# Attention and experts on one core: the third value products of every second unit moved beside the first two, and the first slot's transposes six steps earlier

## The chip, the cores and the metric

The kernel runs on one core of one Trainium2 chip. The metric is device time in microseconds (us) of one execution; less is better. The core has five engines with a queue each: PE (TensorE, matrix products), DVE (VectorE), ACT (ScalarE), POOL (GpSimd) and SP (which here issues DMAs). An instruction waits in its queue for what it needs, and everything behind it in that queue waits too.

## The reference

```python
def _attn_ref(q, k, v, g_q, g_k):              # q, k, v: 8 batches, 12 heads, 448 tokens, 64
    q_n, k_n = (rmsnorm(q, g_q), rmsnorm(k, g_k))
    scores = scale * np.matmul(q_n, k_n.transpose(0, 1, 3, 2))
    scores = scores - np.max(scores, axis=-1, keepdims=True)
    attn = np.exp(scores)
    attn = attn / (np.sum(attn, axis=-1, keepdims=True) + 1e-09)
    return np.matmul(attn, v)
...
def _moe_ref(x, modality_id, w_gate, modality_bias, w1, w2):   # x: 3584 tokens of 768
    logits = x @ w_gate + modality_bias[modality_id]
    e_idx = np.argmax(logits, axis=1)          # one of 8 experts
    ...
    for e in range(E):
        h = np.maximum(x[mask] @ w1[e], 0.0)   # w1: 768 x 1024, w2: 1024 x 768
        out[mask] = gate_w[mask, None] * (h @ w2[e])
```

The output of the attention, with its heads side by side, is the `x` of the second part. All is float32.

## The kernel before

**Attention.** A unit is two heads of one batch, 48 units in all. The 896 rows of its two heads are seven chunks of 128 key rows (j = 0 to 6; chunk 3 holds rows of both heads). The main loop (line 1425) counts steps `n = 7 i + j`: in the step (i, j) PE makes the scores of chunk j of unit i, already transposed (`st`, line 1012: a product in one pass and a second one with the low halves), ACT takes their exponential into `p` (line 1023), and around these two stands the work of other units that a plan assigned to the step. That plan is written out by hand: `put(n, ...)` files a piece of work under a step (lines 1395 to 1423), from the numbers of `PLAN` (line 34). On each engine the instructions run in the order in which the loop issues them.

The pieces that matter here, with the step at which they stand in the main part:

- `sa` (line 981): scores of a later unit (two units ahead), one chunk a step, only for their row maxima; DVE reduces each (line 994). Its PSUM pool has two buffers, so an `sa` needs the reduction of the `sa` two before it.
- `st` has two PSUM buffers too: it needs the exponential of the step two before it.
- `tr` (line 902): transposes of normalised q and k, in steps 3 and 0; ACT casts the result, DVE takes the low half.
- `av` (line 1051): value products. For each of the chunks c = 0, 1, 2 it makes two products, one for each head (chunks c and 4 + c of `p`), each 64 columns of the array wide, side by side. For c = 3 it is one product of full width. `PLAN['av'] = (1, 1, 4, 6)` puts unit u's c = 0 and 1 into step 1 of unit u + 1, c = 2 into step 4, c = 3 into step 6. A float32 product of this kind leaves two records, so c = 0 and 1 together are eight.
- `mt` (line 999), step 1: the row maxima turned for the subtraction.
- `sums` and `gates` (lines 1078, 1087), 32 columns wide, four side by side: `sums` in step 4 of even units, `gates` in step 4 of units 5, 9, 13 and so on, right behind the `av` of that step.
- `xt` (line 1122), step 4: transposes of the finished output of an earlier unit; DVE scales and stores it.
- routing of a finished batch: small DVE instructions (`route`, `route_top` with six of them, line 1163, and others) that a list called `slow` hands out between the steps; `route_top` only in step 4.

**Experts.** Tokens are gathered into slots of 256 of one expert. A slot is a first product with `w1` (`mm1_half`, line 604, tile `ph`, eighteen products for each half column block), a relu, and a second with `w2` (`mm2_step`, `py`). Weights and tokens are split into high and low parts by an ACT cast and a DVE subtraction (`split1`, `w1w`). The first slot starts while attention ends: its tokens are fetched by `xfetch(0)` at n = 312 (line 1534) in four DMAs, and `xturn(0, g)` (line 575) turns them in three groups: DVE transposes 32x32 blocks into a scratch area of `r2w` (one area for all three groups), then ACT casts that to `xh` and DVE subtracts for `xl` (both in `xw`). Each group's cast and subtraction are filed one step behind its transposition. After the loop (line 1566), PE goes on with `mm1_half(0, 0, 0)`, which needs all three groups, the last unit's `av`, and so on.

Of the kernel before, what the change touches and what calls it, by code (L numbers as in the profile page):

```python
# [21 lines left out]
NJ = 7  # L22
NP = H // 2
NU = B * NP
# [42 lines left out]
def kernel(  # L67
# [507 lines left out]
    def xturn(s, g):  # L575
        tt = view(r2w, PW + VW + W, 128, 2, 8, 32) if s == 0 else view(yw, 512 * g, 128, 2, 8, 32)
        V.transpose(out=tt.rearrange("p c g j -> p g c j"),
                    in_=xv(s).rearrange("p g (i c) -> p g c i", c=6)[:, :, 2 * g : 2 * g + 2])
        tt = tt.rearrange("p c g j -> p c (g j)")

        def cast():
            A.copy(xh[:, 2 * g : 2 * g + 2], tt)
            V.tensor_tensor(out=xl[:, 2 * g : 2 * g + 2], in0=tt,
                            in1=xh[:, 2 * g : 2 * g + 2].bitcast(F32), op=ALU.subtract)

        return cast
# [222 lines left out]
    if True:  # L809
# [543 lines left out]
        post, fin = {}, {}  # L1353
# [3 lines left out]
        def at(where, n, fn):  # L1357
            where.setdefault(n, []).append(fn)
# [16 lines left out]
        def put(n, *what):  # L1375
            plan.setdefault(n, []).append(what)

        P = PLAN
        AVJ, XTJ, XTE, SMJ, LAJ, RCJ = (P[x] for x in ("av", "xt", "xte", "sm", "la", "rc"))
        LD0, XRJ = 0, (1, 3, 5)  # L1380
        XTB, XCB, XTB0, XCB0 = (6, 7, 8), (9, 10, 13), (9, 10, 11), (12, 13, 15)
        XLB, XFB = (2, 5), 7
        W3B = (6, 8, 10, 12, 13, 14)
# [11 lines left out]
        for u in range(NU):  # L1395
            for j in range(NJ):
                jj = ((0, 1, 2, 4, 5, 6, 3) if u < P["early"] else (3, 0, 1, 2, 4, 5, 6))[j]
                put(when("sa", u) + j * (P["sastep"] if u == 0 else 1), "sa", u, jj)
            put(when("mt", u), "mt", u)
            if u < NU - 1:  # L1400
                for c in range(4):
                    put(NJ * (u + 1) + (AVJ[c] if u < NU - 2 else min(AVJ[c], 6)), "av", u, c)
            put(xt_at(u), "xt", u)
            if u % 2:
                put(NJ * (u + 1) + (SMJ if u < NP * (B - 2) else P["sml"]), "sums", u - 1)
            if u % 4 == 3:
                put(NJ * (u + 2) + (LAJ if u < NP * (B - 2) else min(LAJ, 4)), "gates", u // 4)
                put(NJ * (u + 2) + (RCJ if u < NP * (B - 2) else min(RCJ, 6)), "recips", u // 4)
            put(when("tk", u), "tr", u, 1)
            put(when("tq", u), "tr", u, 0)  # L1410
            put(when("nq", u), "norm", u, 0)
            put(when("nk", u), "norm", u, 1)
            put(when("sk", u), "sq", u, 1)
            put(when("sq", u), "sq", u, 0)
            if ("rs", u) in P["first"]:
                put(when("rs", u), "rs", u // 3, P["rs0"].get(u, 0), u % 3 + 1)
            elif u > 8 and u % 3 == 2:
                put(when("rs", u), "rs", u // 3, 0, 3)
            if 5 < u < 10:
                put(when("ld", u), "load", u)  # L1420
            elif u > 9 and u % 2 == 0:
                put(when("ld", u) - 1, "load", u, 2, (0,))
                put(when("ld", u) + 1, "load", u, 2, (1,))

        for n in range(P["start"], NJ * NU):
            i, j = divmod(n, NJ)
# [43 lines left out]
            if puts and n >= puts[0][0] and n - lastput[0] >= 3:  # L1470
                lastput[0] = n
                puts.pop(0)[1]()
            if i == NU - 1 and j in XRJ:
                at(post, n + 1, xturn(0, XRJ.index(j)))
            run(pre["A"], n)
            run(pre["V"], n)
            pump(P["rush"][0] if state["rush"] else P["pmpa"][j], j)
# [82 lines left out]
        u, g = NU - 1, NU // 4 - 1  # L1560
# [52 lines left out]
        for s in range(NSTAT):  # L1613
# [32 lines left out]
            for b_ in range(16):  # L1646
                t, j = divmod(b_, 8)
# [100 lines left out]
```

## Time and profile before

| | |
|---|---|
| median of three timed runs | 1034.56 us (1033.47 to 1035.49) |
| profiled execution, its own time | 1032.14 us |
| span of that execution in the trace | 1030.4 us |
| busy: PE / DVE / ACT / POOL | 98% / 72% / 69% / 69% of the span |
| mean granted clock of TensorE | 0.998 of full speed |

Times in rows are microseconds from the start of the span. Attention lasts to about 535 us, the expert slots from there to the end. Matmuls are pipelined, and a record's end is modelled: from start to start is what one costs when the engine is full. A start that stands a few hundredths behind the one ahead belongs to an instruction that is queued behind it.

### The profile page before, as it was taken

The page shows a single profiled execution, that of the slowest core. Times are in us where ns is not written, and L with a number is a line of the kernel's source. Part 1 is how long each engine was busy: PE and PEld are TensorE (multiplying, and loading weights), DVE is VectorE, ACT ScalarE, POOL GpSimd, SP SyncE. Part 2 cuts the span into 40 slices and gives each one's busy share as a digit, 9 for nine tenths or more (in the row PEclk, how much of TensorE's full clock was granted, in tenths as well). Part 3 has the DMA queues.
Part 4 walks back from the last instruction along what each step waited for, and adds up shares of the span by engine and source line. Part 5 has one row for each costly group of instructions (what it writes and reads, how often), then busy time and mean ns, then how long its engine had stood idle before and what let it go on. Part 6 is the DMA issues. An engine that isn't in the chain of part 4 may idle for free. (4 is left out here: it accounts for less than half of the span.)

```text
span 1030.4 us, 18867 instructions
## 1 busy us (share of the span) xinstructions
PE 1013.8 (98%) x6462; PEld 818.4 (79%) x6462; DVE 744.3 (72%) x1260; ACT 709.1 (69%) x1379; POOL 706.2 (69%) x747
## 2 busy tenths in 40 slices
PE   9999999999999999999999999999999999999997
PEld 7655666666666666656559999999999999999995
DVE  6778888887888788887777986855675567656740
ACT  7897999989989899888655555645564455545531
POOL 7887888888798887889866656655544554565351
PEclk9999999999999999999999999999999999999999
DMA  8775667868777686756928516224572342234162
GB/s 205 200 164 125 163 151 177 175 138 186 166 166 159 162 190 150 165 113 138 263 91 270 89 30 201 79 62 124 162 270 71 113 124 82 63 103 123 43 209 92
DMA packets 147900, 148.20 MB, mean 144 GB/s; under 512 B 72702, under 2 KB 137682, under 8 KB 147284
## 3 DMA queue, kind: packets, MB, share of 16 engines
q1 hardware_dynamic: 122398, 105.08, 42.6%
q0 software_dynamic: 25328, 41.82, 12.9%
q8 instruction: 53, 0.87, 0.4%
q14 instruction: 51, 0.42, 0.2%
q10 hardware_dynamic: 70, 0.02, 0.0%
HBM read 150.31 MB, written 33.39 MB: 178 GB/s over the span
## 5 line engine op out<-in xcount | busy, mean ns | idle before, releaser
L609 PE MATMUL ph<-xw,w1w 128*128 128x256 f32 x2016 | 246.2, 283 | 1.7 <-ACT xw L52 1.0
L609 PEld LDWEIGHTS ph<-xw,w1w 128*128 128x128 f32 x2016 | 243.9, 192 | 3.4 <-ACT xw L52 1.2
L52 DVE TENSOR_REDUCE at_hlw<-sa 128x1 f32<-128x448 f32 x336 | 205.2, 619 | 26.0 <-PE sa L991 24.1
L1019 PE MATMUL st<-w1w 128*128 128x448 f32 (+1 forms) x480 | 183.5, 431 | 1.3 <-ACT r2w L52 0.9
L52 POOL DMA_INDIRECT r<-in_moe_w_dram,tb_w x60 | 79.1, 1318 | 56.8 <-DVE w1w L52 41.5
L52 ACT ACTIVATE hhw<-ph 128x512 fp32r<-128x512 f32 x56 | 33.5, 598 | 121.0 <-PE ph L609 121.0
L639 PE MATMUL py<-w2lw,hhw 128*128 128x384 f32 x448 | 113.7, 334 | 0.0
L52 ACT ACTIVATE r2w<-st 128x448 f32<-128x448 f32 x168 | 91.1, 545 | 32.7 <-PE st L1019 25.9
L52 DVE TENSOR_TENSOR w1w<-r,w1w 128x768 fp32r<-128x768 f32 x112 | 104.5, 963 | 11.8 <-ACT w1w L52 10.5
L52 POOL DMA_INDIRECT r2w<-in_moe_w_dram,tb_vi x48 | 48.5, 1010 | 91.7 <-DVE w2lw L52 83.6
L991 PE MATMUL sa<-w1w 128*128 128x448 f32 (+1 forms) x288 | 108.0, 375 | 1.9 <-DVE at_hlw L52 1.5
L52 ACT CAST w1w<-xw 64x448 fp32r<-64x448 f32 x188 | 105.7, 562 | 3.7 <-issue 1.4
L52 DVE TENSOR_TENSOR w2lw<-r2w,w2ha 128x1536 fp32r<-128x1536 f32 x28 | 49.1, 1757 | 81.3 <-ACT w2ha L52 81.3
L1019 PEld LDWEIGHTS st<-w1w 128*128 128x128 f32 (+1 forms) x480 | 86.0, 190 | 24.4 <-issue 11.1
L1019 PE MATMUL st<-w1w,w2ha 65*128 65x448 f32 x288 | 100.4, 369 | 0.0
L52 ACT ACTIVATE at_w2lw<-st 128x448 f32<-128x448 f32 x168 | 90.7, 545 | 12.1 <-PE st L1019 7.0
L52 POOL TENSOR_TENSOR xrw<-r,at_hlw 112x512 f32<-112x512 f32 x95 | 97.6, 1048 | 0.5
L52 POOL TENSOR_TENSOR r2w<-r2w 128x448 f32<-128x448 f32 (+1 forms) x72 | 83.0, 1152 | 21.5 <-DVE r2w L52 15.1
L52 ACT CAST w1w<-r 128x768 fp32r<-128x768 f32 x112 | 95.3, 904 | 0.1
L52 ACT ACTIVATE yw<-py,ltn 128x384 f32<-128x384 f32 x55 | 29.4, 579 | 79.2 <-PE py L639 75.6
L639 PEld LDWEIGHTS py<-w2lw,hhw 128*128 128x128 f32 x448 | 80.9, 188 | 0.0
L52 POOL TENSOR_TENSOR r2w<-r2w,at_w2lw 64x448 f32<-64x448 f32 (+1 forms) x48 | 55.0, 1145 | 30.0 <-DVE r2w L52 15.6
(303 smaller groups left out, 2203.5 us busy)
## 6 DMA issues: line engine op xcount, KB each, us to landing
w1w<-xw SPq DMA_DIRECT2D x216, 112.0 KB
xrw<-xg SPq DMA_DIRECT2D x56, 192.0 KB
xg<-xrw SPq DMA_DIRECT2D x13, 768.0 KB
r<-in_q_dram SPq DMA_DIRECT2D x19, 448.0 KB
r<-in_k_dram SPq DMA_DIRECT2D x19, 448.0 KB
w2ha<-xw SPq DMA_DIRECT2D x72, 112.0 KB
w1w<-w1w SPq DMA_DIRECT2D x48, 112.0 KB
r2w<-in_v_dram SPq DMA_DIRECT2D x24, 224.0 KB
```

Of the source, the lines that this page charges most:

```text
L52: return fn(*a, **kw)
L609: PE.matmul(ps[:, i], lhsT=lt_, rhs=rt_[:, c], start=n == 0, stop=n == 17)
L639: PE.matmul(ps[n][:, :384], lhsT=lt_[:, j, 128 * t : 128 * t + 128], rhs=rt_[:, 384 * n : 384 * n + 384], start=j == 0 and m == 0, stop=j ...
L991: PE.matmul(ps[:, :S], lhsT=t["qq"][r, h, a : a + 128], rhs=t["kk"][h][r], start=True, stop=True)
L1019: PE.matmul(ps[:, :S], lhsT=l, rhs=t["qq"][:, h] if first else t["ql"][0:65, h], start=first and (j != 3 or h == 0), stop=not first and (j ...
```

## The change

The value products of chunk c = 2 of the even units 8 to 44 (nineteen units) are filed under step 1 of the following unit, with those of c = 0 and 1, instead of step 4. The three transpositions of the first slot's tokens, with their casts and subtractions, stand at n = 324, 326, 328 instead of 330, 332, 334: in steps 2, 4 and 6 of unit 46 instead of steps 1, 3 and 5 of unit 47.

```diff
-        LD0, XRJ = 0, (1, 3, 5)
+        LD0, XRN = 0, (324, 326, 328)
...
                 for c in range(4):
-                    put(NJ * (u + 1) + (AVJ[c] if u < NU - 2 else min(AVJ[c], 6)), "av", u, c)
+                    aj = AVJ[1] if c == 2 and u % 2 == 0 and 8 <= u < 45 else AVJ[c]
+                    put(NJ * (u + 1) + (aj if u < NU - 2 else min(aj, 6)), "av", u, c)
...
-            if i == NU - 1 and j in XRJ:
-                at(post, n + 1, xturn(0, XRJ.index(j)))
+            if n in XRN:
+                at(post, n + 1, xturn(0, XRN.index(n)))
```

PE's queue in steps 1 to 4 of unit 23, before (the number behind a name is the program's own; `sa_1` to `sa_4` are for unit 25):

```order
L1061 MATMUL av_3344<-r2w,at_w2lw 64x448 x4
L1002 MATMUL mt_3349<-idn,at_hlw 7x128
L1019 MATMUL st_2_3359<-w1w 128x448 x2
L991 MATMUL sa_1_3362<-w1w 128x448
L1019 MATMUL st_3_3375<-w1w 128x448 x4
L991 MATMUL sa_2_3380<-w1w 128x448
L910 MATMUL tr_0_3382<-idn,xrw 128x112 x4
L1019 MATMUL st_4_3390<-w1w 128x448 x2
L991 MATMUL sa_4_3393<-w1w 128x448
L1061 MATMUL av_3344<-r2w,at_w2lw 64x448 x2
L1127 MATMUL xt_3397<-idn,at_hlw 112x128 x4
```

The same place now:

```order
L1061 MATMUL av_3344<-r2w,at_w2lw 64x448 x6
L1002 MATMUL mt_3351<-idn,at_hlw 7x128
L1019 MATMUL st_2_3361<-w1w 128x448 x2
L991 MATMUL sa_1_3364<-w1w 128x448
L1019 MATMUL st_3_3377<-w1w 128x448 x4
L991 MATMUL sa_2_3382<-w1w 128x448
L910 MATMUL tr_0_3384<-idn,xrw 128x112 x4
L1019 MATMUL st_4_3392<-w1w 128x448 x2
L991 MATMUL sa_4_3395<-w1w 128x448
L1127 MATMUL xt_3397<-idn,at_hlw 112x128 x4
```

Two of the six products have moved up past the score products of three steps, three products for row maxima and two sets of transposes; the output transposes follow `sa_4` directly. On DVE, ACT and POOL nothing moves in these units.

ACT's queue at the end of attention, before, from unit 46's fourth step (`st_3_6264` is unit 46; `st_0_6312` to `st_2_6335` are unit 47):

```order
L52 ACTIVATE r2w<-st_3_6264 128x448
L52 ACTIVATE r2w<-st_4_6272 128x448
L52 CAST w1w<-r_0_158 128x768
L52 ACTIVATE r2w<-st_5_6294 128x448
L52 ACTIVATE r2w<-st_6_6304 128x448
L52 COPY xrw<-av_6239 128x448
L52 ACTIVATE lo_6246<-lo_6246 112x32
L52 ACTIVATE at_w2lw<-st_0_6312 128x448
L52 ACTIVATE at_w2lw<-st_1_6323 128x448
L52 CAST w1w<-r_1_159 128x768
L52 ACTIVATE at_w2lw<-st_2_6335 128x448
L52 CAST xw<-r2w 128x512
```

And now:

```order
L52 CAST xw<-r2w 128x512
L52 ACTIVATE r2w<-st_4_6275 128x448
L52 CAST w1w<-r_0_158 128x768
L52 ACTIVATE r2w<-st_5_6298 128x448
L52 CAST xw<-r2w 128x512
L52 ACTIVATE r2w<-st_6_6310 128x448
L52 COPY xrw<-av_6239 128x448
L52 ACTIVATE lo_6246<-lo_6246 112x32
L52 ACTIVATE at_w2lw<-st_0_6319 128x448
L52 CAST xw<-r2w 128x512
L52 ACTIVATE at_w2lw<-st_1_6332 128x448
L52 CAST w1w<-r_1_159 128x768
```

The three casts of the turned tokens (`xw<-r2w`) stand ahead of exponentials of units 46 and 47 that they stood behind; the exponential of `st_3` is the one ahead of the first row. On DVE the three transpositions move in the same way; now:

```order
L52 TENSOR_TENSOR w1w<-r_0_158,w1w 128x768
L52 STREAM_TRANSPOSE r2w<-xrw 128x8x2x32
L52 TENSOR_TENSOR yw<-xt_6254,rs_171 112x4x128
L52 TENSOR_TENSOR xw<-r2w,xw 128x512
L52 STREAM_TRANSPOSE r2w<-xrw 128x8x2x32
L52 TENSOR_REDUCE ra_6286<-lo_6246 112x4
L52 TENSOR_TENSOR ra_6286<-lo_6246,ra_6286 112x32
L52 SCALAR_TENSOR_TENSOR cd_6287<-ra_6286,ie_132 112x32
L52 TENSOR_REDUCE ra_6286<-cd_6287 112x4
L52 TENSOR_TENSOR zb_134<-i_e,ra_6286 112x32
L52 TENSOR_TENSOR lo_6246<-lo_6246,ra_6286 112x32
L52 TENSOR_TENSOR w1w<-r_0_158,w1w 128x768
```

Before, the first transposition stood behind this second weight subtraction, the output scaling, a partial sum and a count; it has moved up past eleven instructions, to right behind the first weight subtraction.

## Rows read from the trace of the kernel before

**Rows 1.** The page: the span, and busy time of each engine.
```profile
span 1030.4 us, 18867 instructions
PE 1013.8 (98%) x6462; PEld 818.4 (79%) x6462; DVE 744.3 (72%) x1260; ACT 709.1 (69%) x1379; POOL 706.2 (69%) x747
```

**Rows 2.** PE's timeline, unit 21, step 4: start us, us, line, op, out<-in, [idle before <-releaser].
```profile
252.96 0.37 PE L991 MATMUL sa<-w1w 128*128 128x448 f32 x1
253.26 0.97 PE L1061 MATMUL av<-r2w 128*64 128x448 f32 x4
254.16 0.56 PE L1090 MATMUL sm<-at_hhw,wg 128*32 128x448 f32 x1
```

**Rows 3.** PE's timeline, unit 23, step 4.
```profile
274.42 0.37 PE L991 MATMUL sa<-w1w 128*128 128x448 f32 x1
274.72 0.97 PE L1061 MATMUL av<-r2w,at_w2lw 128*64 128x448 f32 x4
275.63 0.65 PE L1127 MATMUL xt<-idn,at_hlw 128*112 128x128 f32 x4
276.03 0.65 PE L1019 MATMUL st<-w1w 128*128 128x448 f32 x2
```

**Rows 4.** PE's timeline near the end of attention: xt between full-width products.
```profile
514.62 0.37 PE L1019 MATMUL st<-w1w,w2ha 65*128 65x448 f32 x1
514.83 0.60 PE L1127 MATMUL xt<-idn,at_hhw 128*112 128x128 f32 x4
515.19 0.64 PE L1019 MATMUL st<-w1w 128*128 128x448 f32 x2
```

**Rows 5.** PE's timeline: a run of eight value products and the last unit's twelve.
```profile
259.25 1.72 PE L1061 MATMUL av<-at_w2lw 128*64 128x448 f32 x8
...
533.81 2.48 PE L1061 MATMUL av<-at_w2lw 128*64 128x448 f32 x12
```

**Rows 6.** DVE's timeline, unit 23 from step 4, and one reduction of unit 40.
```profile
274.76 0.62 DVE L52 TENSOR_TENSOR w1w<-tr,xw 128x448 fp32r<-128x448 f32 x1 [0.33 <-ACT xw L52]
...
275.83 0.18 DVE L52 TENSOR_REDUCE ra<-lo 112x4 f32<-112x32 f32 x1
...
277.53 0.61 DVE L52 TENSOR_REDUCE at_hlw<-sa 128x1 f32<-128x448 f32 x1
...
458.85 0.61 DVE L52 TENSOR_REDUCE at_hlw<-sa 128x1 f32<-128x448 f32 x1
```

**Rows 7.** PE's timeline: the first sa of unit 24 and of unit 41.
```profile
278.50 0.37 PE L986 MATMUL sa<-xw 128*128 128x448 f32 x1
...
459.51 0.47 PE L986 MATMUL sa<-xw,w2ha 128*128 128x448 f32 x1 [0.42 <-DVE at_hlw L52]
```

**Rows 8.** PE's timeline: unit 47's steps 3 and 4, then the first slot's products.
```profile
524.31 1.47 PE L1019 MATMUL st<-w1w 128*128 128x448 f32 x6
...
529.62 1.69 PE L609 MATMUL ph<-xw,w1w 128*128 128x256 f32 x12 [0.40 <-ACT at_w2lw L52]
532.30 0.38 PE L609 MATMUL ph<-xw,w1w 128*128 128x256 f32 x1 [0.98 <-ACT xw L52]
533.02 0.86 PE L609 MATMUL ph<-xw,w1w 128*128 128x256 f32 x5 [0.34 <-DVE xw L52]
```

**Rows 9.** DVE's timeline at the end of attention: two weight subtractions, the first transposition.
```profile
514.36 0.96 DVE L52 TENSOR_TENSOR w1w<-r,w1w 128x768 fp32r<-128x768 f32 x1 [0.36 <-ACT w1w L52]
...
518.67 1.90 DVE L52 TENSOR_TENSOR w1w<-r,w1w 128x768 fp32r<-128x768 f32 x1 [1.40 <-ACT w1w L52]
...
522.11 1.12 DVE L52 STREAM_TRANSPOSE r2w<-xrw 128x512 f32<-128x512 f32 x1
```

**Rows 10.** ACT's timeline: unit 47's first two exponentials, the first cast of turned tokens.
```profile
521.61 0.97 ACT L52 ACTIVATE at_w2lw<-st 128x448 f32<-128x448 f32 x2
...
524.65 0.61 ACT L52 CAST xw<-r2w 128x512 fp32r<-128x512 f32 x1
```

**Rows 11.** SP's queue: the four DMAs that fetch the first slot's tokens.
```profile
499.97 2.02 SPq L563 DMA_DIRECT2D xrw<-xg  x4
```

## Prediction, made before the changed kernel ran

> **What bounds the kernel now.** The first thing to read is the share of busy time [rows 1]: PE is busy for 1013.8 of 1030.4 us, so PE's own stream is the bound and only what shortens that stream, or makes it wait, moves the end. The timeline of PE inside the attention steps comes next, because the change rearranges it. A value product (av, line 1061) runs in a narrow tile 64 columns wide, and the rows show what one visit to that mode costs. In unit 21 a row-maximum product (sa) starts at 252.96, the av behind it at 253.26, the gate product behind that at 254.16 [rows 2]: entering takes 0.30 us from start to start, the pair itself 0.90. In unit 23 there is no gate product, and the visit stands alone between sa and the output transposes (xt): 274.42, 274.72, 275.63, 276.03 [rows 3]. Then DVE and ACT must be read in the same steps: the next product that needs a buffer from them is what takes over when PE gets faster. Last comes the end of attention, where the first expert slot's products (ph) stop three times [rows 8].
>
> **Joining the third chunk.** Each moved pair leaves step 4 of an odd unit and lengthens the av run in step 1 of the same unit. What it adds: the run of eight records lasts 1.72 us, the one run of twelve (unit 47's own, at the end) 2.48 [rows 5], so +0.76. What it removes depends on the neighbour. With gates behind it (units 9, 13 to 45: ten units) the narrow mode is still entered for the gates, so 0.30 stays, and 254.16 - 253.26 = 0.90 goes: net -0.14. With xt behind it (units 11, 15 to 43: nine units) the whole visit goes. 276.03 - 274.42 = 1.61 becomes what full-width products show in unit 47, 514.62 to 514.83 to 515.19 = 0.57 [rows 4]: -1.04, net -0.28. On PE alone this is 10 x 0.14 + 9 x 0.28 = 3.9 us.
>
> No wait comes in with it: the pair needs the exponentials of the unit's sixth and earlier steps, and the score product two places ahead of it in PE's queue needs the last of them already, for its PSUM buffer. What it moves is the rest of the unit. Between step 1 and step 4 everything on PE now stands 0.76 later, and ACT and DVE with it; after step 4 PE is 0.28 ahead again. The price is in those two engines.
>
> **What DVE does with the 0.76.** In unit 23, DVE's subtraction at 274.76 waits for ACT (0.33 idle), ACT's cast for PE; so this chain starts 0.76 later. Behind it come a row maximum, six routing instructions from 275.83, the scaled output and the next row maximum, 277.53 to 278.14, with no gap between them [rows 6]. PE's sa of the next unit needs the buffer that this reduction frees; it starts at 278.50 [rows 7], a slack of 0.36. Now the reduction ends at 278.14 + 0.76 = 278.90, and a reduction that ended at 459.46 let its sa start at 459.51 [rows 6, 7], so sa cannot start before 278.95. That is 0.45 later than before, in place of 0.28 sooner. The trace has the same seven instructions between the two reductions, with a slack of 0.35 to 0.36, in five of the nine units: 11, 15, 23, 27, 35. In the other four (19, 31, 39, 43) routing stands elsewhere: that reduction follows PE's own product directly, with more than twice the slack, so DVE holds nothing there. ACT has four casts between its exponentials of steps 4 and 5 and is late by about 0.14 in two of those four, as I put its rows one behind the other from the delayed start. In the ten units with gates step 4 keeps about the length that it has today in the nine others, and no routing stands in it, so neither engine holds PE.
> Sum: 5 x 0.45 - 4 x 0.28 + 2 x 0.14 - 10 x 0.14 = 2.25 - 1.12 + 0.28 - 1.40 = 0.0 us. Bounds: -3.9 if nothing holds PE; +1.0 if the hold is 0.2 longer than read.
>
> **The transposes, six steps sooner.** Before, ph runs twelve products from 529.62, then stops 0.98 for ACT and 0.34 for DVE on the last third of its transposed block, after 0.40 at its start for an exponential that stood behind two casts of that work; it reaches av at 533.81 [rows 5, 8]. Eighteen products at 0.12 each and the entry of 0.2 would take 2.3 instead of 4.2, so 1.9 goes if the block is ready. It will be: the first transposition follows the weight subtraction that ends at 515.32 and takes 1.12 [rows 9]; the instructions that the order now puts between, laid end to end with their own rows' durations and a cast of 0.61 ahead of each subtraction [rows 10], end the third transposition at 523.6 and its last subtraction near 526, before 529.6.
> The cost is on ACT, whose queue is in order. The third cast now stands ahead of unit 47's second exponential, which ran right behind the first from 521.61 [rows 10]. It waits for the transposition at 523.6, so this exponential starts near 524.1 (2.0 later), and a 0.9 weight cast and the next exponential follow. PE needs them for the six score products that begin at 524.31 [rows 8], the first four and then the last two: about 0.3 and 0.5 of waiting, 0.8 in all. Of it the 0.40 before ph is taken back. ph starts near 529.95 instead of 529.62, and av follows 2.25 later, at 532.2: -1.6, taken as -1.5. Bounds: -2.3 if ACT's delay is all hidden; -0.6 if the second weight subtraction, now at 520.8, takes 1.90 as its row did and not 0.96 as the first [rows 9], since the transposition waits behind it. I take 0.96: POOL has no work there after the move.
> The Trainium skill (SBUF — State Buffer, SBUF: two separate sides) says that DVE and POOL lock each other out of a shared port pair when DVE reads two SBUF inputs. By that rule the 1.90 is a POOL instruction's doing; this trace fits it, and were POOL to meet the moved subtraction, the part would bring the 0.6 named above.
> The moved block's loads are not moved: four parts are issued at 499.97 to 501.99 [rows 11], which left 20 us to the first transposition at 522.11 and leaves 13 now.
>
> **Sum.** 0.0 - 1.5 = -1.5 us, that is 1030.6 beside the profiled execution's 1032.14. That execution lies 2.4 under the median of the three timed runs, 1034.56, so I carry the difference: **1033.1**. What follows after 534 is PE's unbroken stream, and starts earlier as a whole.
>
> **Rivals.** A: DVE does not hold PE, and the whole 3.9 arrives: 1034.56 - 3.9 - 1.5 = 1029.2. For it: over the whole span PE stood for DVE's maxima hardly at all. Against: the slack of 0.36 is read in five units, and 0.76 + 0.28 is three times that. The Trainium skill (TensorEngine Tiling (Array Packing), Key Properties) says that a change of tiling mode drains TensorE; by that rule alone, each mode change saved is a gain, which is this rival. The entry of 0.30 agrees with the drain, but the rule does not see DVE.
> B: the transposes bring nothing, since ACT's delay of 2.0 meets PE in full and takes back the 1.5: 1034.6. For it: PE has two score buffers only. Against: PE needs that exponential at 524.31 and it ended by 522.58 before, a margin of 1.7 to set against the 2.0.
> C, the other side: the block's loads land late. The first transposition would then hold DVE from 515.3, ACT's cast behind it and PE's sixth step of unit 46 behind that. PE's margin there is about 1.4, beyond it each us costs one; the forecast turns to slower by over 0.2% when the last part lands after 515.3 + 1.4 + 3.6 = 520.3, 18 us after its issue: 1037. Against: no DMA wait stands at 522.11, and the queue's traffic is no heavier before.
>
> **How the numbers follow.** Forecast 0.70 (its own range 1031.0 to 1034.6), A 0.17, B 0.08, C 0.05. About 0.2% (2.07 us) is what a measurement of this kernel can tell from no change. The forecast is 1.5 under, and with its own bounds about 0.19 of its 0.70 lies beyond 2.07; with A that makes faster 0.36; slower is C, 0.05; the rest, 0.59, is no difference. The range reaches down over A's value, from 1028.9 to 1034.9.
>
> **What would show it.** Right: in units 12, 16, 24, 28 and 36 the first sa waits for DVE by some 0.7 so that PE's waits on DVE grow by some 4 us in all; the units after 19, 31, 39, 43 come 0.15 to 0.3 sooner; ph runs its eighteen products without the two stops; PE waits some 0.8 for ACT between 524 and 527. Wrong: no such sa waits and attention 3 to 4 us shorter (A); ph still stopping for ACT's cast (B); a DMA as what ended a DVE wait near 515 (C). The forecast also falls if av's run of twelve costs less than 0.76 more than that of eight.

## The result, and the profile after

The changed kernel takes 1039.5 us in the median (sixteen runs, 1035.9 to 1045.7), the kernel before 1034.2 beside it: a ratio of 1.0054, with an interval of 1.0044 to 1.0065. It is slower by some 5.5 us, on the other side of the forecast and beyond the range. Its profiled execution took 1040.24 us, before's 1032.14: 8.1 us between the two traces.

The page after, answering [rows 1]: the span grew by 8.1, PE's busy time by 0.7. PE's idle time (span less busy) grew from 16.6 to 24.0, so nearly all of the loss shows as waiting.

```profile
span 1038.5 us, 18866 instructions
PE 1014.5 (98%) x6462; PEld 818.8 (79%) x6462; DVE 743.7 (72%) x1260; ACT 705.4 (68%) x1379; POOL 708.8 (68%) x747
```

The list of PE's waits (what waited <- what for: us in total, times, longest) names the places. `sa L986`, `ph L609` and the `DMA` lines are new or grown; that of ph for ACT [rows 8] is gone.

```profile
PE ph L609 <- DVE xw L52: 4.2, 2, 2.2
PE sa L986 <- DVE at_hlw L52: 1.8, 6, 0.4
PE tr L910 <- POOL xrw L52: 1.5, 2, 1.2
PE st L1019 <- DMA w1w<-xw: 1.3, 2, 0.8
PE sa L991 <- DMA w1w<-xw: 0.7, 1, 0.7
```

Such a list counts idle time up to a modelled end, so the losses are better taken from starts: the start of one and the same PE instruction in the two timelines, place by place. After less before, in us:

| stretch | change |
|---|---|
| start-up, ahead of the first joined unit | +0.5 |
| joined units with gates: 9, 17, 29, 33, 21 | -0.20 each |
| 13, 25, 41, 45 | -0.15 each |
| 37 and 39 together | -0.86 |
| joined, with routing ahead of the next unit: 11, 15, 23, 27, 35 | +0.55 each, +2.77 |
| 19, 31 and 43 | +0.09, +0.09, 0.0 |
| waits for transfers in units 20 and 21 | +1.94 |
| waits for POOL in units 42 and 44 | +1.98 |
| end of attention: unit 47 +1.21, ph's stops -2.43 | -1.22 |
| start of slot 1 | +5.02 |
| all the rest | -0.5 |
| sum | +8.2 |

The joined units make +0.5 together, near the forecast's 0.0. Three lines were in no sum: 20 and 21, 42 and 44, and slot 1. The second of these is treated below as not, or not surely, the change's; without it and the 0.5 at the start the sum is 5.7, the size of the measured difference.

**The joined units.** PE's timeline after, unit 23 to the start of unit 24, answers [rows 3, 5, 7]. The run of twelve lasts 2.48, as costed; sa to xt to st is 0.56, as costed; then sa at 281.80 starts 0.64 behind the st ahead of it, where 0.20 is usual (278.01 to 278.21).

```profile
273.05 2.48 PE L1061 MATMUL av<-r2w,at_w2lw 128*64 128x448 f32 x12
...
278.01 0.36 PE L991 MATMUL sa<-w1w 128*128 128x448 f32 x1
278.21 0.60 PE L1127 MATMUL xt<-idn,at_hlw 128*112 128x128 f32 x4
278.57 0.65 PE L1019 MATMUL st<-w1w 128*128 128x448 f32 x2
...
281.16 0.37 PE L1019 MATMUL st<-w1w,w2ha 65*128 65x448 f32 x1
281.80 0.47 PE L986 MATMUL sa<-xw 128*128 128x448 f32 x1 [0.28 <-DVE at_hlw L52]
```

DVE's timeline of the same stretch, answering [rows 6], shows the chain that the forecast laid out: the subtraction waits for ACT, and the maximum, six routing instructions, the scaling and the next maximum follow without a gap.

```profile
278.35 0.62 DVE L52 TENSOR_TENSOR w1w<-tr,xw 128x448 fp32r<-128x448 f32 x1 [0.33 <-ACT xw L52]
278.89 0.62 DVE L52 TENSOR_REDUCE at_hlw<-sa 128x1 f32<-128x448 f32 x1
279.43 0.18 DVE L52 TENSOR_REDUCE ra<-lo 112x4 f32<-112x32 f32 x1
...
280.53 0.68 DVE L52 TENSOR_TENSOR yw<-xt,rs 112x512 f32<-112x512 f32 x1
281.13 1.15 DVE L52 TENSOR_REDUCE at_hlw<-sa 128x1 f32<-128x448 f32 x2
```

**The end of attention.** PE's timeline after, answering [rows 8]: the eighteen products run through in 2.3, the stops are gone, and ACT's delay in unit 47 takes half of that gain back.

```profile
529.93 1.91 PE L1019 MATMUL st<-w1w 128*128 128x448 f32 x6 [0.31 <-ACT at_w2lw L52]
...
535.11 2.39 PE L609 MATMUL ph<-xw,w1w 128*128 128x256 f32 x18
537.43 2.48 PE L1061 MATMUL av<-at_w2lw 128*64 128x448 f32 x12
```

**Slot 1.** PE's timeline after. Before, 144 products ran without a stop from 573.46; now the first comes 3.6 later, and two stops of 2.2 and 2.1 follow. The row of before, then those of after:

```profile
573.46 17.43 PE L609 MATMUL ph<-xw,w1w 128*128 128x256 f32 x144
```
```profile
577.09 0.28 PE L609 MATMUL ph<-xw,w1w 128*128 128x256 f32 x1
579.53 1.98 PE L609 MATMUL ph<-xw,w1w 128*128 128x256 f32 x12 [2.17 <-DVE xw L52]
583.56 15.97 PE L609 MATMUL ph<-xw,w1w 128*128 128x256 f32 x131 [2.05 <-DVE xw L52]
```

Followed back, the cause begins at the moved transposes. On DVE the last count of the routing (`cu`) now stands behind the third transposition; before it stood ahead of the first. POOL's copy of that count waits for it, and POOL works in order: behind the copy stand sums of the last units' exponentials, four weight loads and then the gather of slot 1's tokens. DVE's and POOL's timelines after:

```profile
527.68 1.10 DVE L52 STREAM_TRANSPOSE r2w<-xrw 128x512 f32<-128x512 f32 x1
...
529.86 0.53 DVE L52 TENSOR_REDUCE cu<-zb 112x40 f32<-112x200 f32 x1
```
```profile
530.45 1.45 POOL L52 COPY zb<-cu 112x8 f32<-112x8 f32 x1 [5.52 <-DVE cu L52]
...
546.99 0.97 POOL L52 DMA_INDIRECT xrw<-x_d,ltn  x1 [0.30 <-issue]
```

The same rows of before: the copy 8.2 sooner, the gather 4.9 sooner. Not all of this is the wait's: by unit 47 PE itself stands 4.8 later than before, and at the first product of slot 1 it stands 3.6 later. Counted back from that product, the gather comes 1.3 later than before and the fetch below 1.9.

```profile
522.26 0.19 POOL L52 COPY zb<-cu 112x8 f32<-112x8 f32 x1 [2.50 <-DVE cu L52]
...
542.06 0.98 POOL L52 DMA_INDIRECT xrw<-x_d,ltn  x1 [0.30 <-issue]
```

SP stores the gathered tokens (`xg<-xrw`) once they have landed, and fetches them again in parts (`xrw<-xg`). In the same stretch POOL issues slot 2's two gathers and four scatters of routing entries (`l_d<-ltk,posi`, line 1234). Before, the fetch is issued 0.56 ahead of the first scatter and the first transposition of slot 1 starts 7.85 behind the fetch. SP's, POOL's and DVE's timelines of before:

```profile
557.08 1.81 SPq L563 DMA_DIRECT2D xrw<-xg  x4
```
```profile
557.64 0.96 POOL L1234 DMA_INDIRECT l_d<-ltk,posi  x1 [0.30 <-issue]
```
```profile
564.93 2.18 DVE L52 STREAM_TRANSPOSE yw<-xrw 128x512 f32<-128x512 f32 x2 [1.02 <-DMA xrw<-x_d,ltn]
```

After, the fetch is 1.31 behind the first scatter, and the transposition starts 11.44 behind the fetch. The releaser named there is the scatter; a transposition reads what the fetch brings, and the table of slot 1 below is what says that the fetch is late. Between the transposition and slot 1's first product lay 8.5 before (564.93 to 573.46) and lie 3.1 now: of the 5.45 lost, 1.86 is the later issue of the fetch and 3.59 its slower way.

```profile
561.26 0.96 POOL L1234 DMA_INDIRECT l_d<-ltk,posi  x1 [0.30 <-issue]
```
```profile
562.57 1.81 SPq L563 DMA_DIRECT2D xrw<-xg  x4
```
```profile
574.01 2.16 DVE L52 STREAM_TRANSPOSE yw<-xrw 128x512 f32<-128x512 f32 x2 [6.48 <-DMA l_d<-ltk,posi]
```

### The profile page after: what moved, and what is told of

The parts are those of the page before. It is cut to its first block, busy times and chain, and to the rows that moved or that the text cites. A ratio compares the mean times of both kernels' runs of the same rounds, so it can differ in the third digit from the quotient of the medians.

```text
span 1038.5 us, 18866 instructions
## 1 busy us (share of the span) xinstructions
PE 1014.5 (98%) x6462; PEld 818.8 (79%) x6462; DVE 743.7 (72%) x1260; ACT 705.4 (68%) x1379; POOL 708.8 (68%) x747
## 5 line engine op out<-in xcount | busy, mean ns | idle before, releaser
L609 PE MATMUL ph<-xw,w1w 128*128 128x256 f32 x2016 | 246.3, 283 | 4.2 <-DVE xw L52 4.2
L609 PEld LDWEIGHTS ph<-xw,w1w 128*128 128x128 f32 x2016 | 243.9, 192 | 6.0 <-DVE xw L52 4.7
```

The source lines that it names most:

```text
L609: PE.matmul(ps[:, i], lhsT=lt_, rhs=rt_[:, c], start=n == 0, stop=n == 17)
```

## The experiments

Edits are against the kernel before. A kernel "with the join" has the change's value products and before's transposes, one "with the turn" the reverse, unless it is said that it has both.

### Each part alone

`join_only` and `turn_only` have one part of the change each; `join_gates` joins only units with gates, `join_route` only the five with routing.

```diff
+  aj = AVJ[1] if c == 2 and u % 4 == 0 and 8 <= u < 45 else AVJ[c]       # join_gates
+  aj = AVJ[1] if c == 2 and u in (10, 14, 22, 26, 34) else AVJ[c]        # join_route
```

> The join alone, in all nineteen even units; the block's transposes stand where they stood before. From the changed kernel's trace the work itself is worth -0.18 us in each of the ten units with gates, +0.55 in each of the five with the routing's six instructions on DVE, about +0.05 in the other four: together +1.1 us. Theory 1 (the three late arrivals at PE in units 20/21, 42 and 44, 0.94 + 1.6 + 0.8 + 1.2 = 4.5 us, are jitter of DMA landings that any kernel of this shape can show): +0.5 to +2.0 us against the kernel before. Theory 2 (those late arrivals come from the join, which shifts PE against SP's transfers): +4 to +6 us. As predicted on record: 0.0 (-3.9 to +1.0).

> The block transposes six steps sooner alone; the value products as before. Theory 1 (the failed step: the routing's chain on DVE now stands behind the transposes and ACT's casts, POOL waits for its counts, and everything behind that wait in POOL's queue, the gather of slot 1's tokens too, comes late, so that PE stops between slot 0 and slot 1): the two stops in front of slot 0 go (-2.4 us), 1.2 us come back in unit 47, and 4 to 5 us are lost at slot 1's beginning: +2 to +4 us against the kernel before. Theory 2 (the stop at slot 1 needs the shifts of the join as well): -1.5 us, as predicted on record.

> The join only in the ten units with gates behind the value products (u = 8, 12, .. 44); transposes as before. Theory 1 (sums by the kind of the unit: DVE has no routing between the row maxima there, so the saving stands): -1.8 us (ten times -0.18). Theory 2 (the shift against SP's transfers brings late arrivals wherever it is made): +1 to +4 us.

> The join only in the five units in which DVE does the routing's six small instructions between two row maxima (u = 10, 14, 22, 26, 34); transposes as before. Theory 1 (DVE holds the next unit's first scores): +2.7 us (five times 0.55). Rival (DVE's hold is given back later): within 0.5 us of the kernel before.

| kernel | ratio to before | interval |
|---|---|---|
| join_only | 1.0033 | 1.0018 to 1.0048 |
| turn_only | 1.0022 | 1.0006 to 1.0037 |
| join_gates | 1.0001 | 0.9988 to 1.0015 |
| join_route | 1.0036 | 1.0024 to 1.0048 |

Both parts lose, each by its own, and together they make the whole. In join_route's trace the five units cost 0.556 each, 2.78 in all, as in the changed kernel. That settles the hold by DVE: the units alone bring it, without the turn. Its list of PE's waits has six such waits, one of them unit 41's, which before had alone [rows 7]:

```profile
PE sa L986 <- DVE at_hlw L52: 1.8, 6, 0.4
```

join_gates gains 1.7 in its units by its trace, and nothing that can be told in time: in that trace the waits in units 42 and 44 take 1.7 back.

turn_only loses more at slot 1 (7.1 in its trace) than it wins at the end of attention (1.2). It has no joined unit, and the rows show the same order as the changed kernel: fetch (559.48) behind the scatter (557.55), transposition 11.3 behind the fetch. The list of its PE waits, 560 to 600:

```profile
PE ph L609 <- DVE xw L52: 4.3, 2, 2.6
```

### Can slot 1 be mended from the gather

The first theory was the late gather as such. turn_fix issues it ahead of the weight loads; gates_fix adds join_gates. turn_half makes the move three steps instead of six. join_no18 is the join without unit 18's products, which stand in unit 19: it asks whether unit 20's wait for a transfer comes from there.

```diff
+                xgather(1, 0)          # turn_fix: at the loop's end, ahead of wload(0, 1)
+                xgather(1, 1)
...
-        xgather(1, 0)
-        xgather(1, 1)
```
```diff
+        LD0, XRN = 0, (327, 329, 331)                                   # turn_half
+  aj = AVJ[1] if c == 2 and u % 2 == 0 and 8 <= u < 45 and u != 18 else AVJ[c]   # join_no18
```

> The transposes six steps sooner alone, and the two gathers of slot 1's tokens put ahead of slot 0's last four weight loads in POOL's queue (they then are issued 5.2 us sooner: four loads at 1.3 us each); value products as before. Theory 1 (the lost time comes from the late gather and from nothing else): no stop of PE at slot 1's beginning, and what the transposes gave stands: -1.2 us against the kernel before (with the transposes alone, PE stood 2.35 us late at the end of unit 47 and 0.09 us early at slot 0's second product, of which 1.1 us had come before unit 47). Rival (DVE and ACT are late at slot 1 for other reasons, or the weight loads now come 2.6 us late and stop PE in slot 0): +1 to +3 us as with the transposes alone, with the stop elsewhere.

> The transposes three steps sooner than before, not six (steps 327, 329 and 331 of the loop); value products as before. On DVE five of the six routing instructions then stand ahead of the first transposition again, and the count that POOL waits for stands behind the second one, not the third. Theory 1 (what costs is the place of that count ahead of POOL's wait): POOL waits some 3 to 4 us instead of 5.5 and gathers slot 1's tokens about 1 us sooner than with six steps, the stops in front of slot 0 go all the same: -1.0 us, at most +0.5. Rival (any earlier place of the transposes costs the same stop at slot 1): +2 us.

> The join as in the changed kernel but without u = 18 (its work falls in unit 19); transposes as before. In both kernels with the full join, and in none of the four without a join in unit 19, PE waits for transferred halves of q and k in units 20 and 21 (1.0 us, and 0.8 + 0.7 us), and there SP's last move of unit 19 is issued 0.27 us behind POOL's scatter instead of 0.27 us ahead of it. Theory 1 (the join in unit 19 makes SP late against POOL, and the transfers queue behind the scatter): no wait for a transfer in units 20 and 21, +1.0 to +1.5 us against the kernel before. Rival (chance in the landing of transfers, or the shift of PE as such): the waits are there, +2 to +3.5 us.

> The join in the ten gates units alone, the transposes six steps sooner, and slot 1's gathers ahead of slot 0's last weight loads. Theory 1 (all three terms stand by themselves: -1.8 for the join, -1.2 for the transposes): -3.0 us against the kernel before, the fastest of all. Rival (a late landing in the attention or at slot 1 takes it back): -1 to +1 us.

turn_fix: 1.0048 (1.0032 to 1.0065), no better than the turn alone. POOL's gather was issued at 536.99, in turn_only at 543.27, but SP's store waited in its queue behind a store of attention's last output, and the fetch came out at 558.84, still 1.82 behind the scatter (557.02). Here DVE's row names the fetch itself as what it waited for; below it PE's waits, 540 to 600:

```profile
569.98 2.15 DVE L52 STREAM_TRANSPOSE yw<-xrw 128x512 f32<-128x512 f32 x2 [6.69 <-DMA xrw<-xg]
```
```profile
PE ph L609 <- DVE xw L52: 4.4, 2, 2.4
```

gates_fix: 1.0037 (1.0023 to 1.0050), the same stop. turn_half: 1.0017 (1.0006 to 1.0028). Its fetch is 0.5 ahead of the scatter and slot 1 has no stop; but PE loses 3.4 in unit 47, waiting for ACT's exponentials, so that the end of attention is 1.2 later, not 1.2 sooner. join_no18: 1.0013 (1.0004 to 1.0022). No wait in units 20 and 21, but one of 2.8 in unit 19, for a move that landed 8.5 us behind its issue, though the nearest scatters stand 3.8 ahead of that and 1.9 behind; it stays unexplained. By PE's starts that one wait cost unit 19 4.7, since the granted clock was 0.72 in the 6 us from 231 on.

### What the fetch waits behind

Two theories stood: the fetch is slow behind slot 2's gathers, or behind the scatters. keep_early lets the store and the gathers go before attention's stores, so that the fetch is ahead of both; gates_keep adds join_gates; put_first lets each of the two gathers change places with the scatter behind it; puts_late puts both gathers first and files the scatters later, so that the fetch is ahead of the scatters; gates_puts_late adds join_gates. All have the turn. join_again is join_only once more.

```diff
-        if s not in (0, 2):
+        if s not in (0, 1, 2):          # keep_early: store of slot 1 right behind its gathers
...
+        route_put(B-2, 0)               # put_first
         xgather(2, 0)
...
+                at(beat, 17, lambda: route_put(B - 2, 3))    # puts_late: last one of four
```

> The transposes six steps sooner alone, slot 1's gathers ahead of slot 0's last four weight loads on POOL, and SP's store of these tokens (xkeep) ahead of the last two stores of x_d in SP's queue, which held it back before (549.99 to 551.03 us); value products as before. In the ten kernels seen so far, the fetch of slot 1's tokens is issued 1.7 to 1.8 us ahead of POOL's second gather for slot 2 in the six without the stop at slot 1, and 0.03 to 0.7 us behind it in the four with the stop; from the fetch to the first transposition it is 7.5 to 8.1 us there and 10.7 to 11.5 here. Theory 1 (the fetch queues behind that gather): here it is issued some 4 us ahead of both gathers, no stop at slot 1, -1.3 us against the kernel before. Rival (the stop comes from the transposes' places themselves, whatever the fetch does): +2 to +4 us.

> The transposes six steps sooner alone; on POOL each of slot 2's two gathers changes places with the scatter of routing entries behind it, so that the second gather is issued 1.3 us later and all else stands as with the transposes alone; value products as before. Theory 1 (whether the fetch of slot 1's tokens is issued ahead of that second gather decides): the fetch then is 0.6 us ahead, it lands some 3 us sooner, and at most a small stop is left at slot 1: -1 us against the kernel before, at most +1. Rival (the late gather of slot 1 as such, or the two weight loads of 562 us, decide): the stop of 4 us stays, +2 to +4 us.

> The join in the ten gates units alone, with the transposes six steps sooner and slot 1's gathers and store put ahead as in the kernel with the early store. Theory 1 (the terms add up): -1.8 for the join and -1.3 for the transposes, -3.1 us against the kernel before, the fastest of all. Rival (a late landing at slot 1 or in the attention takes it back): -1 to +1 us.

> The kernel with the join alone once more, for one more profile. Theory 1 (late landings around units 19 to 21, where DMA moves without a pause, are chance, and the join only leaves PE without cover): the waits there differ from the first profile's (1.0 us at one place) by more than 0.5 us, or are at another unit. Rival (they belong to the join): 1.0 us at the first scores of unit 20 or 21 again. The sums by units are the same to 0.02 us: -0.20 and -0.14 in gates units, +0.55 in the five with the routing.

> The transposes six steps sooner alone; on POOL, in slot 0, both gathers for slot 2 stand right behind the two weight loads and the four scatters of routing entries behind them (the first by one place, the last behind slot 0's first output scatter); value products as before. Theory 1 (a transfer of SP that is issued behind such a scatter lands late): the fetch of slot 1's tokens is issued about 0.3 us ahead of the first scatter again, though behind both gathers; it lands as in the kernel before (7.5 to 8.1 us to the first transposition), no stop at slot 1, -1.2 us against the kernel before. Rival (the gather ahead of the fetch decides): the stop of some 4 us stays, +2 to +4 us.

> As the kernel with the late scatters, and the join in the ten gates units. Theory 1 (the terms add up): -1.8 and -1.2, so -3.0 us against the kernel before. Rival (as above): +1 to +2 us.

put_first speaks against the gathers: the fetch, at 559.12, is ahead of both of slot 2's gathers (559.57, 562.95) and behind one scatter (558.30), and it is late: 11.45 to the transposition. puts_late is the counterpart, and a weaker one. SP's, POOL's and DVE's timelines: the fetch stands behind one gather, ahead of the other and of the scatter, and is used 9.4 behind its issue; PE does not stop.

```profile
559.77 2.02 SPq L563 DMA_DIRECT2D xrw<-xg  x4
```
```profile
559.01 0.96 POOL L52 DMA_INDIRECT xrw<-x_d,ltn  x1 [0.30 <-issue]
560.28 0.97 POOL L52 DMA_INDIRECT xrw<-x_d,ltn  x1 [0.30 <-issue]
561.55 1.83 POOL L1234 DMA_INDIRECT l_d<-ltk,posi  x1 [0.30 <-issue]
```
```profile
569.13 2.18 DVE L52 STREAM_TRANSPOSE yw<-xrw 128x512 f32<-128x512 f32 x2 [2.58 <-DMA xrw<-xg]
```

But 9.4 is hardly better than the 9.6 and 9.5 of turn_again and after_again below, whose fetch is behind the scatter, and PE came later to slot 1 here, having waited 1.5 in slot 0 for the chain behind a late activation (the last section). So with no scatter ahead something still slows the fetch by 0.6 (gates_puts_late) or 1.5, perhaps the second gather, 0.5 behind it where it was 1.8 behind before; that was not tried. Without PE's 1.5 there might be a small stop.

All twenty traces, by the order of issue at slot 1, in us (fetch's start less that of the first scatter; the fetch to the first transposition; what PE lost, from its starts):

| kernels | fetch less scatter | to transposition | lost |
|---|---|---|---|
| before, before_scatter, turn_half, the six with the join and no turn | -0.6 to -0.5 | 7.5 to 8.1 | 0 |
| keep_early, gates_keep (fetch not waited for) | -4.9 | 11.1 | 0 |
| puts_late, gates_puts_late | -1.8, -1.7 | 9.4, 8.4 | 0 |
| turn_again, after_again | +0.4 | 9.6, 9.5 | 3.7 |
| put_first | +0.8 | 11.4 | 2.0, PE itself having waited 1.4 in slot 0 |
| after, turn_fix, gates_fix, turn_only | +1.3 to +1.9 | 10.7 to 11.4 | 5.0 to 7.1 |

Every kernel whose fetch follows the scatter stops, none whose fetch precedes it does. Where the fetch is waited for and a trace has all its semaphore events, the last of its four parts lands 7.2 to 7.8 behind the fetch with the scatter behind, 9.2 to 11.1 with it ahead. The stop hangs on the fetch's late issue as well: from fetch to slot 1's first product there are 16.3 to 16.4 in the first row of the table, 15.5 in turn_again and after_again, 13.9 to 14.5 in the last row. The highest losses (turn_only, gates_fix) and part of the 3.7 are the clock's, as the last section shows. In times: puts_late 1.0005 (0.9995 to 1.0015) and keep_early 1.0011 (0.9998 to 1.0023), put_first 1.0045 (1.0031 to 1.0058). With the stop taken away the turn costs nothing that can be told; neither does it gain. gates_keep 1.0009 (0.9996 to 1.0021) and gates_puts_late 1.0020 (1.0004 to 1.0036) show that neither sum of the good parts beats the kernel before. join_again, with one run, took 1038.3 beside 1034.3 and had the wait for a transfer in unit 20 again.

### The wait for transfers in units 20 and 21

In unit 19, too, a scatter stands beside SP's transfers: a move of the low halves (`w1w<-w1w`, line 923) that PE needs in unit 20 and the loads of q, k and v behind it. Before, SP issued the move 0.27 ahead of the scatter, in the changed kernel 0.27 behind it. SP's and POOL's timelines after, then before:

```profile
236.22 0.56 SPq L923 DMA_DIRECT2D w1w<-w1w  x1
```
```profile
235.95 0.96 POOL L1234 DMA_INDIRECT l_d<-ltk,posi  x1 [0.16 <-issue]
```
```profile
234.63 0.55 SPq L923 DMA_DIRECT2D w1w<-w1w  x1
```
```profile
234.90 0.96 POOL L1234 DMA_INDIRECT l_d<-ltk,posi  x1 [0.15 <-issue]
```

join_scatter is the join with that one scatter a step later; before_scatter is before with it a step sooner.

```diff
-            if puts and n >= puts[0][0] and n - lastput[0] >= 3:
+            if puts and n >= puts[0][0] and n - lastput[0] >= 3 and n != 137:      # join_scatter
+            if puts and n >= puts[0][0] and (n - lastput[0] >= 3 or n == 136):     # before_scatter
```

> The full join with the transposes as before, and one single scatter of routing entries, the fourth of those between units 17 and 19, one step of the loop later (two POOL products, 1.8 us). Theory 1 (SP's last move of unit 19, issued 0.27 us behind that scatter, and the loads behind it land 2 to 3 us late): the move is issued ahead of the scatter and lands in 2.2 to 2.7 us, no wait for a transfer in units 20 and 21, +1.0 to +1.7 us against the kernel before instead of the +1.9 to +3.4 of the join alone. Rival (the order of the two is only a sign of something else): the waits are there as before (0.5 to 1.0 us at two places, 2.0 to 2.7 us in all).

> The kernel before with that single scatter one step of the loop earlier (1.4 us), so that it is issued ahead of SP's last moves of unit 19; nothing else is changed. Theory 1: the last move lands in 4 us or more instead of 2.4, the value loads behind it in 9 us or more instead of 7.0, though PE may have cover for it there: 0 to +2 us. Rival: 2.2 to 2.7 us and 6.7 to 8.1 us as in all kernels without the full join, 0 us.

Time from issue to landing, from the trace's semaphore events, of that move and of the three loads behind it:

| kernels | move less scatter, us | move | q | k | v |
|---|---|---|---|---|---|
| before and eleven others | -0.3 | 2.2 to 2.7 | 5.1 to 6.1 | 6.0 to 7.7 | 6.7 to 8.3 |
| join_scatter | -1.4 | 2.1 | 4.7 | 5.8 | 7.2 |
| turn_only | +0.1 | 3.0 | 6.3 | 7.7 | 8.5 |
| join_only, join_again, after, after_again | +0.3 | 4.1 to 4.3 | 7.7 to 7.9 | 9.0 to 9.2 | 9.8 to 10.3 |
| before_scatter | +1.2 | 4.5 | 7.1 | 8.2 | 8.8 |

(join_no18 is not in it: there the move came after the wait in unit 19, 4.2 behind the scatter.) With the scatter behind the move again, join_scatter has no wait for a transfer between 228 and 262; join_only has one of 1.0 there. before_scatter, with no join at all, has the late landing (and the slack to cover it: 1.0005, 0.9993 to 1.0016). So the order of the two makes the lateness, taken away and brought about by moving the scatter alone. join_scatter's time is 1.0015 (1.0005 to 1.0026), against join_only's 1.0033: better by about what the waits cost, though on another chip and with intervals that overlap.

The Trainium skill (DMA: Bandwidth & Descriptors, Queues, rings and completion order) says that each DMA engine takes turns between the queues it has work for, packet by packet. Sharing by turns does not account for the delay here. In the changed kernel POOL's queue has 32 packets between 236 and 241, which take 0.9% of the DMA engines' time, and from 240 to 241, with the three loads still to land and the move until 240.5, the engines are busy for 0.22 of the time. In before_scatter, at the like place (238.4 to 239.4), it is 0.19; in before 0.99 there, in join_scatter 1.13 from 240 to 241. So behind the scatter the transfers nearly stand still for a while, and not for want of DMA engines.

### The two stops once more

turn_again and after_again repeat turn_only and the changed kernel beside each other.

> The kernel with the early transposes alone once more, for a second profile. If the stop at slot 0's xt belongs to the conditions of the run and not to the edits, it shows here as in the five others (1.4 to 1.8 us) or it stays out as in this kernel's first profile, and the time moves by up to 3 us between the two; the stop at slot 1 (fetch issued behind the first scatter) stays in either case: 3.5 to 4.5 us, less where PE comes late to it. If it belongs to the edits: no stop at xt, the same stop at slot 1, +2.3 us against the kernel before as in the first runs.

> The changed kernel once more. Theory 1 (the causes found are in the program's order): waits for a transfer in units 20 and 21 of 1 to 2 us in all, next units held by 0.55 us five times, the fetch of slot 1's tokens behind the first scatter and a stop at slot 1: +4 to +7 us against the kernel before. Rival (chance in that one profile): no wait in units 20 and 21, or no stop at slot 1.

1.0027 (1.0004 to 1.0050) and 1.0080 (1.0055 to 1.0105). Both stop at slot 1, once, for 2.0, with the fetch only 0.4 behind the scatter, and lose 3.7 there; after_again waits in units 20 and 21 again:

```profile
PE sa L991 <- DMA w1w<-xw: 0.6, 1, 0.6
PE st L1019 <- DMA w1w<-xw: 0.4, 1, 0.4
```

## Why the prediction was wrong

**PE's own sums were right.** "+0.76" for the run of twelve is 2.48 in the row after; the visit of 1.61 became 0.56; a unit with gates gained 0.15 to 0.20, put at 0.14. None of the failed steps is a PE duration.

**The hold by DVE was right, its size 0.10 short.** 0.55 in place of 0.45 in each of exactly the five units named. The forecast priced the start of the waiting sa, 278.95; the record behind a wait also lasts 0.47 in place of 0.37, in the row after as in [rows 7]. ACT's delay "by about 0.14 in two of those four" was mis-sized too: units 19 and 31, put at -0.28 + 0.14, came 0.09 later, so ACT took 0.37. In unit 19, behind the four casts, two exponentials start at 236.92 and take 0.98 together, and PE's next score product starts at 237.52. Unit 43 stayed at 0.0 in place of -0.28. The five held units and these three lost some 1.3 more than forecast, and the units with gates and 37 and 39 gained some 0.8 more: +0.5 over the units 9 to 46 where 0.0 stood, inside the bounds, and so near in part by luck.

**"No wait comes in with it" was wrong.** The sentence looked at what the moved pair itself reads. What it missed is what the 0.76 carries along: the issue of a transfer on SP follows work that is 0.76 later, POOL's scatter does not follow it as far, and they stood 0.27 apart. Against the scatter the move came 0.54 later, the order of the two was turned round, and the transfer landed 2 to 3 us later in a place with no slack. It cost 1.9 in the profile, 1.5 to 1.8 in three others. The forecast asked this of the moved block's loads (rival C) and not of any transfer of the joined units.

**The end of attention was right, and nearly of its size.** ph's stops went (2.43), ACT's delay cost unit 47 1.21 where 0.8 was put, net -1.2 for -1.5. (In the forecast's own terms ph starts at 529.62 + 0.8 - 0.4 = 530.02, not "near 529.95"; the 0.07 changes nothing.) Rival C did not come: the fetched block was there. On the shared port pair, which the prediction drew from the Trainium skill (SBUF — State Buffer, SBUF: two separate sides), the trace agrees: POOL waited for `cu` while the moved subtraction ran, and the row after, 526.09, has 0.95, the shorter of the two durations in [rows 9].

```profile
526.09 0.95 DVE L52 TENSOR_TENSOR w1w<-r,w1w 128x768 fp32r<-128x768 f32 x1
```

**"What follows after 534 is PE's unbroken stream, and starts earlier as a whole" is the step that failed most.** It was right of the order in PE's own queue and said nothing of DVE, POOL and SP. The order of instructions in the section on the change showed that the transposes passed DVE's count, and the forecast even used "POOL has no work there after the move" as a good thing: POOL had none because it stood waiting for that count, with a gather behind it. What that count held up reached PE by way of the fetch, issued later and landing more slowly behind a scatter. The cost is 5.0 in the profile (3.7 to 7.1 in the other traces with the order unmended, put_first's 2.0 apart): about four times the gain of 1.2.

**Units 42 and 44 stay open.** A list is read there (line 379) only when POOL's last scatter has landed, and PE waits 1.2 or so for it. Twelve of the twenty traces have that wait with 1.2 to 1.3, four with 0.5 to 0.6; before's trace has none. Without it, before's profiled execution is 2.4 under its median, about the wait's size in the two units, which speaks for chance. So do two pairs of runs of one and the same program: turn_only has none and turn_again 1.2, join_only 0.6 and join_again 1.3. But all eleven kernels with joined units have 0.5 or more, and of the nine without, five. So the join may make it more frequent; it may be why join_gates' 1.7 never appeared in its time. No run tells this.

## What to carry to other kernels

An edit that delays one engine's instructions by a fraction of a microsecond can turn round the issue order of two DMAs of different queues; where an indirect scatter of small entries is one of them, ask of each pair that lies that close which goes first, and whether the other's user has slack. For a step that is moved past an instruction, follow that instruction to its readers and on through everything queued behind them in order, up to the next transfer, even where the bound engine's own queue looks unbroken. A gain at the bound engine's end of a phase counts only when the next phase's first operand is known to come sooner by as much.

## What was not expected of the hardware

**A scatter slows transfers that were issued after it on another queue.** Landing of a small move went from 2.2 to 2.7 us to 4.1 to 4.5, of the loads behind it from 7 to 8 us up to 10; a fetch that was used 7.5 to 8.1 us behind its issue took 9.5 to 11.4. An issue 0.3 or 0.5 ahead of the scatter has the low values. For the move this is shown both ways, by moving the scatter alone; for the fetch puts_late leaves a part open. What in the scatter does this wasn't tried; that its packets fill the DMA engines is ruled out, since these stood at 0.2.

**PE's clock fell after the stops, in some traces.** The two levels are 0.50 and 1.00 of full speed, and a mean between them is a mixture. Windows of turn_only (stretch, its length, busy time of PE, PEld, DVE, ACT and POOL, granted clock, DMA share, GB/s): after a stretch in which PE was busy 3.41 of 6 us, the granted clock of the next was 0.50, the lower of the two levels throughout, and this is how its slot 1 lost 7.1, where its two stops are 4.3.

```profile
572.00:578.00 6.00, 3.41 (x21) 3.10 (x21) 5.95 (x9) 4.96 (x8) 0.26 (x1) 0.94 0.51 110
578.00:584.00 6.00, 4.24 (x19) 3.94 (x19) 5.11 (x10) 3.46 (x5) 4.78 (x5) 0.50 0.43 113
```

The changed kernel's own trace has PE busy 2.39 of the same second stretch with a clock of 1.00; turn_again, with one stop of 2.0, had 0.72 there, after_again 0.87; gates_fix had 0.68. So such a stop costs more than itself in some executions and not in others; what decides it stays open.

**ACT started late on finished products on some chips.** In all eight traces of the two sets of runs from keep_early to before_scatter in the order above, each set on a chip of its own, an activation of slot 0 started up to 3 us later than PE's rows would let it; in none of the other twelve traces, the same edits among them. PE then waited for what hangs on it: 0.5 in the three of the eight without the turn, 1.4 to 1.8 in the five with it. Row of keep_early, then of turn_only, ACT's timeline:

```profile
551.19 0.60 ACT L52 ACTIVATE hhw<-ph 128x512 fp32r<-128x512 f32 x1 [5.91 <-remote]
```
```profile
546.34 0.60 ACT L52 ACTIVATE hhw<-ph 128x512 fp32r<-128x512 f32 x1 [3.11 <-PE ph L609]
```

The lateness isn't the edits' doing, since join_only and join_again are one program; whether it is the chip's or the hour's isn't told. What it costs is in part the turn's. So it lowers what puts_late and keep_early could show of the turn's gain.
